# Second-pass w2 parts written one by one into w1's places of the first pass, block 0's last tiles spread over the first slot, w1 stores and weight sums at other times

## The chip, the cores and the metric

One Trainium2 chip; the kernel runs on one of its cores. The metric is the device time of one execution in microseconds (us), the median of several runs.

## The reference, cut to what matters

```python
# attention: 4 batches x 8 heads, 576 positions, head size 64
scores = where(mask, q @ k.T / 8, -1e9)   # heads 0-3: last 32 positions; heads 4-7: every 4th of the last 128
x = (softmax(scores) @ v)                 # gathered to [2304, 512]
# mixture of 4 experts, all used, weighted by p
p = domain_probs / (domain_probs.sum(-1, keepdims=True) + 1e-9)
for e in range(4):
    h = maximum(x @ w1[e], 0)             # [2304, 512] @ [512, 1024]
    out += p[:, e:e+1] * (h @ w2[e])      # [2304, 1024] @ [1024, 512]
```

## The kernel before, in words

The tokens lie in three blocks of 768 (`TB`), the 4 x 1024 hidden columns in 16 units `u` of 256. Every product is done in split precision: an operand is a high part in fp32r and a low part (the rest), and three matmuls (high by high, low by high, high by low) stand for one. The first layer uses a Strassen-like scheme with seven products per unit: w1 of a unit is turned into seven 256 x 128 pieces (A11, A12, A22 and the sums S1 to S4), x into seven pieces (B11 to T4).

**First pass.** While attention is still computing blocks 1 and 2, `experts` takes block 0 through all 16 units. For a unit, `w1_split` makes the high and low parts of A11, A12, A22 (tiles `g1h`, `g1l`, two buffers each; ScalarE makes the high part, GpSimd the low part), `w1_sums` makes the sums in place on GpSimd, `w1_late` splits the sums (`g2h`, `g2l`, one buffer each) and fetches the raw w1 of unit u+2 (tag `r1`, two buffers). `w2_late` splits the unit's w2 (raw tile `r2`, parts `w2h`, `w2l`) and fetches the next raw w2. `mm1_a` and `mm1_b` do the seven products, `mm2` the second layer: six output tiles of 128 tokens by 512, six matmuls each, in four PSUM banks, added up with the weight p by `weigh_out` (VectorE, L593). `keep_w1` (L218) stores the seven split pieces of a unit to DRAM in four DMAs, for the second pass. All these loads and stores are issued by SyncE's one queue, in program order, and an issue whose source or place isn't ready holds all behind it. ScalarE, VectorE, GpSimd and TensorE also take their instructions in program order.

**Second pass.** `second_pass` takes blocks 1 and 2 through the units in pairs: 16 groups of (pair, block), and a loop of 17 *slots*. A slot has seven steps b = 0 to 6. In it stand the first layer of group n (14 products `m1`, L501, six matmuls each, from pieces loaded back by `load_w1`, L709) and, between them, the second layer of group n-1 (seven products P1 to P7 by `m2`, L825). The seven w2 parts of a pair are made by the generator `w2_parts`: it fetches two raw w2 tiles (L847), and at each step makes a sum on GpSimd (L861 to L874), a high part on ScalarE (L855) and a low part on GpSimd (L856). `background(b)` takes one such step in most steps b, and one step of `w1_again`, which does for units 0 and 1 what `keep_w1` did for the others (sum L895, high part L897, low part L898, store L900).

In slot 0 there is no group before, so in its steps 0, 1 and 2 the last six tiles of block 0's second layer are done, two each. After step 2 `first_over` closes the pools of the first pass, and opens in their space the pool `late`, with the seven w2 parts, the raw w2 tiles, the places of the h pieces and the accumulators of blocks 1 and 2; the steps of the first `w2_parts` stand in b = 3 to 6, two in each.

Of the kernel before, what the change touches and what calls it, by code (L numbers as in the profile page):

```python
# [48 lines left out]
def kernel(  # L49
# [119 lines left out]
    def w1_sums(u):  # L169

        r = raw1[u]
        a11, a12 = r[:, 0:2, 0:128], r[:, 2:4, 0:128]
        a21, a22 = r[:, 0:2, 128:256], r[:, 2:4, 128:256]
        flush()
        tt = nc.gpsimd.tensor_tensor
        tt(out=a22, in0=a21, in1=a22, op=ALU.add)
        yield
        tt(out=a21, in0=a11, in1=a21, op=ALU.subtract)
        yield
        tt(out=a11, in0=a22, in1=a11, op=ALU.subtract)  # L180
        yield
        tt(out=a12, in0=a12, in1=a11, op=ALU.subtract)
        yield

    def w1_late(u):
        r = raw1.pop(u)
        gh = wp.tile([128, 4, 2, 128], F32R, tag="g2h", name="g2h")
        gl = wp.tile([128, 4, 2, 128], F32R, tag="g2l", name="g2l")
        ready1[u] += (gh, gl)
        for i, (n, c, f) in enumerate(  # L190
            (("S2", 0, 0), ("S1", 2, 128), ("S3", 0, 128), ("S4", 2, 0))
        ):
            v = (slice(None), slice(c, c + 2), slice(f, f + 128))
            split(gh[:, i], gl[:, i], r[v], nc.gpsimd if u > 2 else nc.vector)
            a_op[u, n] = (gh[:, i], gl[:, i])
            yield
        if u + 2 <= LAST:
            fetch_w1(u + 2)

    def w2_late(u):  # L200
        r = raw2.pop(u)
# [7 lines left out]
            fetch_w2(u + 1)  # L209


    def keep_w1(u):

        kept[u] = dram.tile([NO, 128, 2, FU], F32, name=f"w1_{u}")
        g1h, g1l, g2h, g2l = ready1.pop(u)
        for side, tiles in enumerate(((g1h, g2h), (g1l, g2l))):
            for at, t in zip((slice(0, 3), slice(3, NO)), tiles):
                nc.sync.dma_start(  # L218
                    out=kept[u][at, :, side, :].rearrange("n p f -> p n f"),
                    in_=t.bitcast(F32).rearrange("p n c f -> p n (c f)"),  # L220
                )

    b_op = {}

# [396 lines left out]
    def experts(begin):  # L621
# [35 lines left out]
        for i, (u, _) in enumerate(visits):  # L657
            end = u == LAST
            need(w1_late, u)
            keep_w1(u)  # L660
            yield from mm1_b((u, 0))
            if end:
                for n in ("T3", "T4"):
                    for j in (4, 5):
                        prepare(x_part, j, n)
                break
            prepare(w1_late, u + 1)
            if u + 2 <= LAST:
                prepare(w1_split, u + 2)
                prepare(w1_sums, u + 2)  # L670
            need(w1_split, u + 1)
            opening = mm1_a((u + 1, 0))
            yield next(opening)
            need(w2_late, u)
            yield from mm2((u, 0), False, False, 1)
            begin()
            yield from opening
            if u + 1 == LAST:

                assert "m1" in gate  # L680
                need(x_sums, 5)
                for n in ("T2", "T1"):
                    for j in (4, 5):
                        prepare(x_part, j, n)
            yield from mm2((u, 0), False, False, 0)
            if u + 2 <= LAST:
                prepare(w2_late, u + 2)
# [151 lines left out]
                    out=out[tt * 128:(tt + 1) * 128, d], in_=acc_t[g.m][:, at, d]  # L839
                )  # L840

    def w2_parts(pair):

        raw = []
        for u in pair:
            r = pools["late"].tile([128, 2, DM], F32, tag="r", name="r", bufs=2)
            nc.sync.dma_start(out=r, in_=w2_rows(u))  # L847
            raw.append(r)
        yield
        one, two = slice(0, DM // 2), slice(DM // 2, DM)  # L850
        b11, b12, b21, b22 = (r[:, :, d] for r in raw for d in (one, two))

        def split2(n, src):
            h, l = w2s[n][:, 0], w2s[n][:, 1]
# [12 lines left out]
        split2("P3", b22)  # L867
        yield
        tt(out=b12, in0=b22, in1=b12, op=ALU.subtract)
        split2("P7", b12)  # L870
        yield
        split2("P2", b21)
        yield
        tt(out=b21, in0=b21, in1=b11, op=ALU.add)  # L874
        split2("P4", b21)
        yield

    def w1_again(u):
# [9 lines left out]
        for n, src, one, two, op in (  # L888
# [17 lines left out]
    def second_pass(tiles):  # L906
# [11 lines left out]
        def first_over():  # L918
# [7 lines left out]
            for n in ORDER:  # L926
                w2s[n] = late.tile([128, 2, 2, DM // 2], F32R, name=f"w2_{n}")
            for at, names in enumerate((("S1", "S4"), ("S2", "A12"))):
                place = tuple(
                    late.tile([128, 2, TH], F32R, name=f"h{at}{i}") for i in ("h", "l")  # L930
                )
                for n in names:
                    h_places[n] = place

        g = h = w2_steps = None
        for n in range(len(groups) + 1):
            h, g = g, Group(n) if n < len(groups) else None

# [9 lines left out]
            def mm2_(b):  # L948
                if h:
                    m2(h, ORDER[b])  # L950
                elif b < 3:
                    for _ in range(2):
                        next(tiles)
                if n == 0 and b == 2:
                    assert next(tiles, 0) == 0
                    first_over()

            def background(b):
                nonlocal w2_steps
# [462 lines left out]
```

## Time and profile before

| what | us |
|---|---|
| median of 3 runs | 828.93 (828.52 to 831.21) |
| the profiled execution | 833.97 |
| its span, first to last instruction | 832.2 |
| TensorE busy | 800.9 (96%) |
| VectorE busy | 600.9 (72%) |
| GpSimd busy | 368.0 (44%) |
| ScalarE busy | 347.3 (42%) |
| mean granted TensorE clock | 0.984 |

Times in the profile count from the first instruction of the profiled execution. An idle time in square brackets stands before the instruction of its row, with what ended it. TensorE is the engine that is nearly always busy, so its idle time and the stretches in which its granted clock is under 1.00 are what to look for.

### The profile page before, as it was taken

To read this page: it belongs to the slowest core of one execution; us is meant where nothing else is said; L and a number is where in the kernel's file an instruction comes from. 1 tells how busy PE (TensorE), PEld (TensorE's weight loads), DVE (VectorE), ACT (ScalarE), POOL (GpSimd) and SP (SyncE) were. 2 spreads that over 40 slices of the span, in tenths; PEclk is the share of its full clock that TensorE was granted. 3 is DMA by queue.
4 is the path that set the end of the run, shared out by engine and by line. 5 is a ranking of instruction groups with operands and counts; after the bars stand their busy time and mean duration, and the time that the engine had idled before them with its cause. 6 is when DMAs were issued, how large, how long until landed. Compare 5 with 4: busy or idle time off the path is not lost.

```text
span 832.2 us, 17899 instructions
## 1 busy us (share of the span) xinstructions
PE 800.9 (96%) x7020; PEld 752.2 (90%) x7020; DVE 600.9 (72%) x1249; ACT 347.3 (42%) x707; POOL 368.0 (44%) x367
## 2 busy tenths in 40 slices
PE   8999799999999999599999999999999999999997
PEld 5878688888888889499999999999999999999997
DVE  4787456666665786367887777777886887877977
ACT  2555255454445534233443443442443432433432
POOL 4446578887776883330431631640520511502500
PEclk9999899999999999879999999999999999999999
DMA  7755675877555845535456456455454454454432
GB/s 221 233 154 136 221 249 174 261 218 218 174 172 171 278 153 179 179 94 176 127 171 197 145 156 206 139 158 173 125 171 124 125 172 124 125 178 127 128 108 95
DMA packets 101230, 140.08 MB, mean 168 GB/s; under 512 B 7561, under 2 KB 61705, under 8 KB 101147
## 3 DMA queue, kind: packets, MB, share of 16 engines
q1 hardware_dynamic: 100731, 138.51, 53.8%
q8 instruction: 56, 0.92, 0.4%
q10 hardware_dynamic: 416, 0.43, 0.1%
q14 instruction: 27, 0.22, 0.1%
HBM read 104.83 MB, written 34.08 MB: 167 GB/s over the span
## 4 chain that ended last, share of the span: by engine, by line
PE 84%; POOL 5%; DVE 5%; issue 3%; ACT 2%; DMA 1%; DVEq 0%; POOLq 0%; SPq 0%; ACTq 0%
PE m1x L501 24%; PE m L612 15%; PE m1y L501 15%; PE x L825 14%; PE y L825 11%; PE po L415 2%; POOL w_P L856 2%; PE sc L326 2%; DMA r<-w 1%; DVE acc L593 1%; PE wt L1177 1%; PE pt L395 1%; DVE xr L253 1%; DVE g L807 1%; POOL r L895 1%
## 5 line engine op out<-in xcount | busy, mean ns | idle before, releaser
L856 POOL TENSOR_TENSOR w_P<-r,w_P 128x512 fp32r<-128x512 f32 x56 | 75.9, 1357 | 259.8 <-PE m1y L501 164.0
L593 DVE SCALAR_TENSOR_TENSOR acc<-m,pn,acc 128x512 f32<-128x512 f32 x90 | 67.1, 748 | 39.2 <-PE m L612 39.1
L612 PE MATMUL m<-w2h,hh 128*128 128x512 f32 x192 | 77.9, 406 | 5.5 <-DVE acc L593 5.5
L807 DVE SCALAR_TENSOR_TENSOR g<-g 128x768 f32<-128x768 f32 x64 | 78.1, 1220 | 0.5
L612 PE MATMUL m<-w2l,hh 128*128 128x512 f32 x192 | 75.7, 394 | 0.0
L593 DVE SCALAR_TENSOR_TENSOR acc<-x,pn,acc 128x256 f32<-128x256 f32 x174 | 73.0, 473 | 0.9 <-PE x L825 0.9
L791 DVE TENSOR_TENSOR h0l<-g,h0h 128x768 fp32r<-128x768 f32 x32 | 36.7, 1146 | 45.2 <-ACT h0h L779 45.2
L593 DVE SCALAR_TENSOR_TENSOR acc<-y,pn,acc 128x256 f32<-128x256 f32 x138 | 58.0, 474 | 13.7 <-PE y L825 13.1
L501 PE MATMUL m1x<-xh_B,s_A 128*128 128x384 f32 x256 | 66.2, 340 | 0.0
L825 PE MATMUL x<-w_P,xh_T 128*128 128x256 f32 x384 | 61.5, 282 | 0.0
L825 PE MATMUL y<-w_P,h0h 128*128 128x256 f32 x384 | 61.3, 282 | 0.0
L612 PE MATMUL m<-w2h,hl 128*128 128x512 f32 x192 | 60.3, 395 | 0.4 <-DVE hl L525 0.4
L501 PE MATMUL m1y<-xh_B,s_S 128*128 128x384 f32 x192 | 49.9, 341 | 8.8 <-ACT g L763 8.8
L855 ACT ACTIVATE w_P<-r 128x512 fp32r<-128x512 f32 x56 | 34.9, 627 | 53.4 <-POOL r L861 21.1
L825 PEld LDWEIGHTS y<-w_P,h0h 128*128 128x128 f32 x384 | 54.2, 189 | 0.1
L825 PEld LDWEIGHTS x<-w_P,xh_T 128*128 128x128 f32 x384 | 54.3, 189 | 0.0
L501 PE MATMUL m1x<-xh_T,s_S 128*128 128x384 f32 x192 | 50.2, 342 | 3.5 <-DVE g L761 2.1
L612 PEld LDWEIGHTS m<-w2h,hh 128*128 128x128 f32 x192 | 36.3, 189 | 14.9 <-DVE acc L593 7.6
L138 POOL TENSOR_TENSOR g2l<-r,g2h 128x256 fp32r<-128x256 f32 x52 | 39.4, 770 | 22.3 <-ACT g2h L141 22.0
L771 ACT ACTIVATE g<-m1x 128x384 f32<-128x384 f32 x32 | 15.7, 492 | 74.0 <-PE m1x L501 74.0
L501 PEld LDWEIGHTS m1x<-xh_B,s_A 128*128 128x128 f32 x256 | 46.2, 190 | 0.1
L138 POOL TENSOR_TENSOR g1l<-r,g1h 128x256 fp32r<-128x256 f32 x45 | 34.0, 762 | 23.7 <-ACT g1h L141 23.7
(203 smaller groups left out, 2263.6 us busy)
## 6 DMA issues: line engine op xcount, KB each, us to landing
s_S<-w SPq DMA_DIRECT2D x128, 256.0 KB, 2.9
r<-w SPq DMA_DIRECT2D x49, 512.0 KB, 4.3
s_A<-w SPq DMA_DIRECT2D x96, 256.0 KB, 3.0
v_s<-vw SPq DMA_DIRECT2D x48, 192.0 KB, 4.8
w<-g2h SPq DMA_DIRECT2D x14, 512.0 KB, 5.4
w<-g2l SPq DMA_DIRECT2D x14, 512.0 KB, 6.2
w<-g1h SPq DMA_DIRECT2D x14, 384.0 KB, 4.8
w<-g1l SPq DMA_DIRECT2D x14, 384.0 KB, 5.9
```

What stands on the lines that cost most here:

```text
L138: lo_eng.tensor_tensor(out=lo, in0=src, in1=hi.bitcast(F32), op=ALU.subtract)
L326: nc.tensor.matmul(banks[swap][o:o + QB, i * KB:(i + 1) * KB], q_s[h, c0:c0 + QB], k_s[h, c0:c0 + KB], start=True, stop=True, skip_group_c ...
L415: nc.tensor.matmul(po[k][64 * j:64 * j + 64, o:o + QB], v_s[rows, j, 2 * i + half, :], ts_[rows, c:c + QB], start=True, stop=True,)
L501: nc.tensor.matmul(bank, w[:, k], x[:, k], start=(first and k == 0 and i == 0), stop=(last and k == 1 and i == 2), skip_group_check=True,)
L593: nc.vector.scalar_tensor_tensor(out=acc, in0=po, scalar=pn[:, tt, e:e + 1], in1=acc, op0=ALU.mult, op1=ALU.add,)
L612: nc.tensor.matmul(po, h, w, start=(n == 0 and x == 0), stop=(n == 3))
L771: copy(out=g.h[v, 0][:, 1], in_=to, func=AF.Copy)
L791: nc.vector.tensor_tensor(out=l, in0=source(g, n), in1=h.bitcast(F32), op=ALU.subtract)
L807: nc.vector.scalar_tensor_tensor(out=g.h[n], in0=g.h[one], scalar=0.0, in1=g.h[two], op0=ALU.max, op1=op)
L825: nc.tensor.matmul(to, h_places[factor][low][:, c, t * 128:(t + 1) * 128], w[:, x, c], start=begins and k == 0 and t != 1, stop=k == len(o ...
L855: nc.scalar.activation(out=h, in_=src, func=AF.Copy)
L856: nc.gpsimd.tensor_tensor(out=l, in0=src, in1=h.bitcast(F32), op=ALU.subtract)
```

## The change

- **Places.** The pool `wp` (raw and split weights of the first pass) stays open to the end, and only `fp` is closed. The two raw w2 tiles of a pair take the two `r1` buffers of raw w1; the parts are written one by one to `r2` (P1), `g2h` (P5), `g2l` (P6), the `w2h` and `w2l` of the unit before the last (P3, P7) and of the last (P2, P4). The places of the h pieces become `g1h` and `g1l`.
- **Fetch.** The raw w2 of the first pair is fetched by `w1_late` of units 14 and 15, where no w1 is left to fetch; later pairs in steps 2 and 3 of an odd slot.
- **First slot.** One tile of block 0 at each of b = 1 to 6, `first_over` after b = 6; w2 parts at b = 0 to 4, the last two in steps 0 and 1 of slot 1.
- **Stores.** A unit's `g1h` and `g1l` are stored when `w1_sums` begins, its `g2h` and `g2l` before `mm1_b` (for unit 2 after it).
- **Sums.** In `w2_parts` a sum is made at the end of the step before the one that splits it; in `w1_again` a step of its own lies between sum and split.

```diff
+    wp = ctx.enter_context(tc.tile_pool(name="wp", bufs=1))
     first_pass = ExitStack()
     fp = first_pass.enter_context(tc.tile_pool(name="fp", bufs=1))
-    pools = {}
-    wp = first_pass.enter_context(tc.tile_pool(name="wp", bufs=1))
...
     def w1_sums(u):
         flush()
+        keep_w1(u, False)
...
     def w1_late(u):
         if u + 2 <= LAST:
             fetch_w1(u + 2)
+        else:
+            fetch_w2_half(pairs2[0][u + 2 - NU])
...
-            keep_w1(u)
+            if u > 2:
+                keep_w1(u, True)
             yield from mm1_b((u, 0))
+            if u == 2:
+                keep_w1(u, True)
...
+    W2_PLACES = {
+        "P1": "r2", "P5": "g2h", "P6": "g2l", "P3": "w2h", "P7": "w2l", "P2": "w2h", "P4": "w2l",
+    }
...
+    def fetch_w2_half(u):
+        r = wp.tile([128, 2, DM], F32, tag="r1", name="r", bufs=2)
+        nc.sync.dma_start(out=r, in_=w2_rows(u))
+        raw_pair.append(r)
...
         split2("P1", b11)
+        tt(out=b11, in0=b12, in1=b11, op=ALU.subtract)
         yield
-        tt(out=b11, in0=b12, in1=b11, op=ALU.subtract)
         split2("P5", b11)
+        tt(out=b11, in0=b11, in1=b22, op=ALU.subtract)
         yield
-        tt(out=b11, in0=b11, in1=b22, op=ALU.subtract)
         split2("P6", b11)
...
     def w1_again(u):
             if op is not None:
                 tt(out=src, in0=one, in1=two, op=op)
+                yield
...
             def mm2_(b):
                 if h:
                     m2(h, ORDER[b])
-                elif b < 3:
-                    for _ in range(2):
-                        next(tiles)
-                if n == 0 and b == 2:
+                elif b:
+                    next(tiles)
+                if n == 0 and b == 6:
                     assert next(tiles, 0) == 0
                     first_over()
...
             def background(b):
-                if n == 0:
-                    if b == 3:
-                        w2_steps = w2_parts(pairs2[0])
-                        next(w2_steps)
-                    for _ in range(2 if b > 2 else 0):
-                        next(w2_steps, 0)
-                elif odd and b == 2 and q + 1 < len(pairs2):
-                    w2_steps = w2_parts(pairs2[q + 1])
-                    next(w2_steps)
-                elif not odd and b > 0 or odd and b < 2:
+                if n == 0 and b < 5 or n and not odd and b > 0 or odd and b < 2:
                     next(w2_steps, 0)
+                elif odd and q + 1 < len(pairs2):
+                    if b in (2, 3):
+                        fetch_w2_half(pairs2[q + 1][b - 2])
+                    elif b == 6:
+                        w2_steps = w2_parts()
```

**ScalarE in slot 0**, from the copy of the first product on (g and m1x, m1y are first-layer results and their banks, w2_P1 a w2 part, r its raw tile, xh_B22 the place of an h piece). Before:

```order
L759 ACTIVATE g_4715<-m1x_4714 128x384
L763 ACTIVATE g_4752<-m1y_4751 128x384
L765 ACTIVATE g_4752<-m1x_4742 128x384
L759 ACTIVATE g_4842<-m1x_4841 128x384
L1002 ACTIVATE g_4752<-g_4752 128x768
L771 ACTIVATE g_4715<-m1x_4742 128x384
L855 ACTIVATE w2_P1_4822<-r_4860 128x512
L855 ACTIVATE w2_P5_4823<-r_4860 128x512
L779 ACTIVATE xh_B22_0_934<-g_4715 128x768
L763 ACTIVATE g_4881<-m1y_4880 128x384
L855 ACTIVATE w2_P6_4824<-r_4860 128x512
```

And now:

```order
L765 ACTIVATE g_4719<-m1x_4718 128x384
L872 ACTIVATE w2_P1_4737<-r_4490 128x512
L769 ACTIVATE g_4742<-m1y_4741 128x384
L771 ACTIVATE g_4742<-m1x_4728 128x384
L872 ACTIVATE w2_P5_4768<-r_4490 128x512
L872 ACTIVATE w2_P6_4797<-r_4490 128x512
L765 ACTIVATE g_4801<-m1x_4800 128x384
L1015 ACTIVATE g_4742<-g_4742 128x768
L777 ACTIVATE g_4719<-m1x_4728 128x384
L872 ACTIVATE w2_P3_4828<-r_4643 128x512
L785 ACTIVATE xh_B22_0_934<-g_4719 128x768
L769 ACTIVATE g_4853<-m1y_4852 128x384
```

P1 stood behind six other instructions and now stands behind one; P5 and P6 now stand ahead of the copy of the eighth product (g_4801).

**SyncE's queue about units 2 and 3** (w1_2 is unit 2's store in DRAM, r1 and r2 raw w1 and w2). Before:

```order
L125 DMA r1_1500<-w1 128x4x256
L218 DMA w1_2_1504<-g1h_1306 128x3x256
L218 DMA w1_2_1504<-g2h_1450 128x4x256
L218 DMA w1_2_1504<-g1l_1307 128x3x256
L218 DMA w1_2_1504<-g2l_1451 128x4x256
L311 DMA v_s_1518<-vw 64x2x384 x2
L311 DMA v_s_1521<-vw 64x2x384 x2
L301 DMA q_s_1524<-qT 128x384
L302 DMA k_s_1525<-kT 128x2x224
L301 DMA q_s_1528<-qT 128x384
L302 DMA k_s_1529<-kT 128x2x224
L129 DMA r2_1532<-w2 128x2x512
```

And now:

```order
L125 DMA r1_1503<-w1 128x4x256
L314 DMA v_s_1516<-vw 64x2x384 x2
L314 DMA v_s_1519<-vw 64x2x384 x2
L304 DMA q_s_1522<-qT 128x384
L305 DMA k_s_1523<-kT 128x2x224
L304 DMA q_s_1526<-qT 128x384
L305 DMA k_s_1527<-kT 128x2x224
L129 DMA r2_1530<-w2 128x2x512
L221 DMA w1_3_1608<-g1h_1532 128x3x256
L221 DMA w1_3_1608<-g1l_1533 128x3x256
L221 DMA w1_2_1328<-g2h_1453 128x4x256
L221 DMA w1_2_1328<-g2l_1454 128x4x256
```

Unit 2's four stores stood ahead of unit 3's raw w2; two of them now stand a few issues before these rows (ahead of one v, q and k), two behind the raw w2, after unit 3's first two.

**GpSimd in slot 4** (r is raw w2, r1 the raw w1 of `w1_again`, again its split piece). Before:

```order
L856 TENSOR_TENSOR w2_P1_4822<-r_5688,w2_P1_4822 128x512
L861 TENSOR_TENSOR r_5688<-r_5688 128x2x256
L856 TENSOR_TENSOR w2_P5_4823<-r_5688,w2_P5_4823 128x512
L895 TENSOR_TENSOR r1_5599<-r1_5599 128x2x128
L898 TENSOR_TENSOR again_6007<-r1_5599,again_6007 128x256
L864 TENSOR_TENSOR r_5688<-r_5688,r_5690 128x2x256
L856 TENSOR_TENSOR w2_P6_4824<-r_5688,w2_P6_4824 128x512
```

And now:

```order
L912 TENSOR_TENSOR r1_5598<-r1_5598 128x2x128
L873 TENSOR_TENSOR w2_P1_4737<-r_5687,w2_P1_4737 128x512
L877 TENSOR_TENSOR r_5687<-r_5687 128x2x256
L916 TENSOR_TENSOR again_5960<-r1_5598,again_5960 128x256
L873 TENSOR_TENSOR w2_P5_4768<-r_5687,w2_P5_4768 128x512
L880 TENSOR_TENSOR r_5687<-r_5687,r_5734 128x2x256
L873 TENSOR_TENSOR w2_P6_4797<-r_5687,w2_P6_4797 128x512
```

A sum stood at the head of a step, right before the high part on ScalarE and the low part on GpSimd that are made from it; now it stands at the end of the step before, and the low part of `again` comes a step after its sum.

## Rows read from the trace of the kernel before

**Rows 1.** The page: busy time by engine, and TensorE in 40 slices.

```profile
PE 800.9 (96%) x7020; PEld 752.2 (90%) x7020; DVE 600.9 (72%) x1249; ACT 347.3 (42%) x707; POOL 368.0 (44%) x367
...
PE   8999799999999999599999999999999999999997
```

**Rows 2.** Windows in slot 0: length, busy PE, PEld, DVE, ACT, POOL, clock, DMA.

```profile
340.50:349.50 9.00, 0.20 (x2) 0.00 (x0) 0.39 (x1) 2.37 (x4) 3.60 (x3) 0.77 0.55 194
349.50:363.40 13.90, 11.76 (x43) 10.74 (x44) 7.69 (x7) 5.65 (x10) 11.52 (x9) 0.53 0.23 77
```

**Rows 3.** Timeline of TensorE in slot 0: start, duration, instruction, [idle before <-releaser].

```profile
349.51 1.01 PE L501 MATMUL m1y<-xh_B,s_S 128*128 128x384 f32 x2 [8.81 <-ACT g L763]
```

**Rows 4.** Timelines of SyncE's queue and of ScalarE in slot 0.

```profile
337.96 0.94 SPq L847 DMA_DIRECT2D r<-w  x2
...
344.38 0.63 ACT L855 ACTIVATE w_P<-r 128x512 fp32r<-128x512 f32 x1 [6.23 <-DMA r<-w]
```

**Rows 5.** Chain of waits in slots 0 and 1: start, duration, what ran.

```profile
320.87 1.06 PE m1x L501 x6
321.93 2.76 PE m L612 x12
...
365.60 2.14 PE y L825 x18
```

**Rows 6.** Timelines of ScalarE and VectorE at slot 0's first products.

```profile
324.94 0.49 ACT L759 ACTIVATE g<-m1x 128x384 f32<-128x384 f32 x1 [1.68 <-DVE xl_T L138]
...
326.07 0.54 DVE L761 TENSOR_TENSOR g<-m1x,g 128x384 f32<-128x384 f32 x1
```

**Rows 7.** GpSimd's L861 (ns min/median/max); GpSimd's and VectorE's timelines in slot 5.

```profile
L861 POOL TENSOR_TENSOR r<-r x8: 1262/1885/1886, 346.4 to 763.8; 128x512 f32<-128x512 f32 x8
...
484.12 0.75 POOL L898 TENSOR_TENSOR again<-r,again 128x256 fp32r<-128x256 f32 x1 [0.53 <-ACT again L897]
...
485.69 2.05 DVE L807 SCALAR_TENSOR_TENSOR g<-g 128x768 f32<-128x768 f32 x1
```

**Rows 8.** Windows in the first pass, unit 2 to 3, columns as in Rows 2.

```profile
93.40:98.70 5.30, 0.01 (x1) 0.00 (x0) 1.51 (x3) 3.09 (x8) 2.39 (x2) 0.77 0.21 81
98.70:103.20 4.50, 4.49 (x12) 3.90 (x13) 1.36 (x2) 0.00 (x0) 3.88 (x6) 0.52 0.41 129
```

**Rows 9.** Timeline of SyncE's queue ahead of unit 3's raw w2.

```profile
80.14 0.51 SPq L218 DMA_DIRECT2D w<-g1h  x1
...
83.79 4.02 SPq L311 DMA_DIRECT2D v_s<-vw  x4
...
90.01 9.51 SPq L129 DMA_DIRECT2D r<-w  x2
```

**Rows 10.** Timelines of VectorE, ScalarE and TensorE about that stall.

```profile
90.76 0.56 DVE L542 TENSOR_TENSOR s<-m1y,s 128x384 f32<-128x384 f32 x1 [0.38 <-PE m1y L501]
...
95.60 1.15 ACT L141 ACTIVATE w2h<-r 128x512 fp32r<-128x512 f32 x2 [9.55 <-DMA r<-w]
...
98.71 0.80 PE L612 MATMUL m<-w2h,hh 128*128 128x512 f32 x1 [5.30 <-DVE acc L593]
```

**Rows 11.** The page, DMA issues: count, KB each, median us to landing.

```profile
r<-w SPq DMA_DIRECT2D x49, 512.0 KB, 4.3
...
w<-g2l SPq DMA_DIRECT2D x14, 512.0 KB, 6.2
```

**Rows 12.** Waits from 400 us on: total us, times, longest.

```profile
ACT w_P L855 <- POOL r L861: 18.4, 7, 2.6
...
ACT again L897 <- POOL r L895: 15.3, 6, 3.5
...
PE m1x L501 <- DVE g L761: 5.0, 4, 1.5
```

**Rows 13.** Window over slots 4 to 7, columns as in Rows 2.

```profile
450.00:571.00 121.00, 116.01 (x812) 114.45 (x811) 90.71 (x147) 50.05 (x88) 46.78 (x40) 1.00 0.54 166
```

**Rows 14.** Waits over the whole span: total us, times, longest.

```profile
ACT w2h L141 <- DMA r<-w: 10.5, 2, 9.5
```

More of the change, by code (lines that the diff above doesn't have):

```diff
@@ L83 @@
     )
+    pools = {}
+    wp = ctx.enter_context(tc.tile_pool(name="wp", bufs=1))
     first_pass = ExitStack()
     fp = first_pass.enter_context(tc.tile_pool(name="fp", bufs=1))
-    pools = {}
-    wp = first_pass.enter_context(tc.tile_pool(name="wp", bufs=1))
     ident = const.tile([128, 128], F32, name="ident")
@@ L209, in w2_late, with keep_w1 @@
             fetch_w2(u + 1)
[L212 to L221, printed above, removed]
+    def keep_w1(u, late):
+        if not late:
+            kept[u] = dram.tile([NO, 128, 2, FU], F32, name=f"w1_{u}")
+        at = slice(3, NO) if late else slice(0, 3)
+        for side, t in enumerate(ready1[u][2:] if late else ready1[u][:2]):
+            nc.sync.dma_start(
+                out=kept[u][at, :, side, :].rearrange("n p f -> p n f"),
+                in_=t.bitcast(F32).rearrange("p n c f -> p n (c f)"),
+            )
     b_op = {}
@@ L840, in m2, with w2_parts @@
                 )
[L842 to L849, printed above, removed]
+    W2_PLACES = {
+        "P1": "r2", "P5": "g2h", "P6": "g2l", "P3": "w2h", "P7": "w2l", "P2": "w2h", "P4": "w2l",
+    }
+    raw_pair = []
+    def fetch_w2_half(u):
+        r = wp.tile([128, 2, DM], F32, tag="r1", name="r", bufs=2)
+        nc.sync.dma_start(out=r, in_=w2_rows(u))
+        raw_pair.append(r)
+    def w2_parts():
         one, two = slice(0, DM // 2), slice(DM // 2, DM)
-        b11, b12, b21, b22 = (r[:, :, d] for r in raw for d in (one, two))
+        b11, b12, b21, b22 = (r[:, :, d] for r in raw_pair for d in (one, two))
+        raw_pair.clear()
         def split2(n, src):
+            if n not in w2s:
+                tag = W2_PLACES[n]
+                w2s[n] = wp.tile(
+                    [128, 2, 2, DM // 2], F32R, tag=tag, name=f"w2_{n}",
+                    bufs=2 if tag[0] == "w" else 1,
+                )
             h, l = w2s[n][:, 0], w2s[n][:, 1]
@@ L867, in w2_parts @@
         split2("P3", b22)
+        tt(out=b12, in0=b22, in1=b12, op=ALU.subtract)
         yield
-        tt(out=b12, in0=b22, in1=b12, op=ALU.subtract)
         split2("P7", b12)
@@ L872, in w2_parts @@
         split2("P2", b21)
+        tt(out=b21, in0=b21, in1=b11, op=ALU.add)
         yield
-        tt(out=b21, in0=b21, in1=b11, op=ALU.add)
         split2("P4", b21)
@@ L925, in first_over @@
             pools["late"] = pools["acc"] = late
-            for n in ORDER:
-                w2s[n] = late.tile([128, 2, 2, DM // 2], F32R, name=f"w2_{n}")
             for at, names in enumerate((("S1", "S4"), ("S2", "A12"))):
                 place = tuple(
-                    late.tile([128, 2, TH], F32R, name=f"h{at}{i}") for i in ("h", "l")
+                    wp.tile([128, 2, TH], F32R, tag=f"g1{i}", name=f"h{at}{i}", bufs=2)
+                    for i in ("h", "l")
                 )
@@ L933, in first_over @@
                     h_places[n] = place
-        g = h = w2_steps = None
+        g = h = None
+        w2_steps = w2_parts()
         for n in range(len(groups) + 1):
@@ L960, in background @@
                 q, odd = divmod(n, 2)
-                if n == 0:
-                    if b == 3:
-                        w2_steps = w2_parts(pairs2[0])
-                        next(w2_steps)
-                    for _ in range(2 if b > 2 else 0):
-                        next(w2_steps, 0)
-                elif odd and b == 2 and q + 1 < len(pairs2):
-                    w2_steps = w2_parts(pairs2[q + 1])
-                    next(w2_steps)
-                elif not odd and b > 0 or odd and b < 2:
-                    next(w2_steps, 0)
+                if n == 0 and b < 5 or n and not odd and b > 0 or odd and b < 2:
+                    next(w2_steps, 0)
+                elif odd and q + 1 < len(pairs2):
+                    if b in (2, 3):
+                        fetch_w2_half(pairs2[q + 1][b - 2])
+                    elif b == 6:
+                        w2_steps = w2_parts()
                 if n > 2 and again and next(again[0], 0) == 0:
```

## The prediction

> **What bounds the kernel now.** I read the busy times first, then the windows, then the timelines of the places where TensorE idles. TensorE is busy 800.9 us of 832.2 and no other engine over 72% (PEld is its own weight load), so the work of TensorE is the floor; the 31 us in which it idles, and the time that it runs at half clock, are all that a change of order can win [rows 1]. In the slices the reader is to see a 7 in the fifth (83 to 104 us) and a 5 in the seventeenth (333 to 354 us) among nines. Both lie where the diff works, and the waits show a third place there that is too short for a slice.
>
> *Slot 0, the hand-over between the passes.* From 340.5 us on TensorE works 0.2 us in 9.0, and for the 13.9 us behind that its granted clock is 0.53, about 1.2 GHz in place of 2.4 [rows 2]. It waits for ScalarE's copy L763 [rows 3]. ScalarE was free, but ahead of that copy in its queue stands the high part of P1, and this waits for raw w2, which SyncE issues only at 337.96, when the first pass's space is given up; it is there at 344.4 [rows 4]. The parts behind it wait for GpSimd's sums in turn, with the copies that TensorE needs in between.
>
> *Unit 2 to 3 of the first pass.* TensorE idles 5.30 us from 93.4 and then runs 4.5 us at a clock of 0.52 [rows 8]. It waits for a PSUM bank, the bank for VectorE, VectorE for ScalarE's `hh`, and ScalarE for unit 3's raw w2: the copy L141 idled 9.55 us, to 95.60, because of that load [rows 10]. The load was issued at 90.01, behind the four stores of unit 2 (80.14 to 83.79), four issues of v (4.02 us) and two each of q and k [rows 9].
>
> *Slots 4 to 7.* TensorE idles 5.0 us in four stalls, all before a product that waits for VectorE's L761 [rows 12], at clock 1.00 throughout [rows 13]. VectorE is late there because ScalarE had waited for GpSimd sums: 18.4 us in all for L861, 15.3 us for L895 [rows 12].
>
> **The change part by part.** The sum is made against the profiled execution, 833.97 us; its median runs are 5.0 us shorter, and I take the saving off the median as it is.
>
> *A. Slot 0.* From the end of the product at 340.5 to where the clock is full again, at 363.4, 22.9 us pass. In them lie four products and P1: 4 x 1.06 + 2.14 = 6.4 us at full clock [rows 2, 3, 5]. So 16.5 us are to be won at most. What must be there instead: raw w2 is fetched by `w1_late` of units 14 and 15, and the later of these stands ahead of unit 15's `mm1_b`, five products or 5.3 us before slot 0 [rows 5]; at 4.3 us a load [rows 11] both halves are in before slot 0's first copy at 324.94 [rows 6]. No place of P1 to P7 is late either: the last one to be stored, `g2l` of unit 15, lands 6.2 us after its issue [rows 11], about 1 us into slot 0, and P6 is due some 10 us later. P2 and P4 wait for the last tile, but stand in slot 1, and are read only in its steps 5 and 6.
>
> Two new waits I see. First, four tiles (4 x 1.38, from 2.76 for two) stood between the second product and the fourth; now one does [rows 5]. The fourth adds into a bank that VectorE's L761 must have read, and L761 needs ScalarE's first copy, which ran only at 324.94 since it waited for x parts whose space it takes [rows 6]. So L761 ends at 324.94 + 0.49 + 0.54 = 326.0 or a little later, and TensorE is there at 320.87 + 3 x 1.06 + 1.38 = 325.4: a new stall of 0.7 us. Second, P5 and P6 stand on ScalarE ahead of the copy that frees the bank of the ninth product. Their chain starts when P1's high part ends, 0.63 us behind the first copy, at 326.1: low part, sum, P5's high part, low part, sum, P6's high part, copy. With the four GpSimd operations at 1.26 us, two high parts (0.63), the copy (0.49) and some 0.1 us for each hand-over it ends at 333.4; with 1.88 us each [rows 7] at 335.9. TensorE wants the bank at 326.1 + 5 x 1.06 + 2 x 1.38 = 334.2. I take 0.3 us, nearer to the short end, since slot 0 has no second layer of a group before, whose VectorE work surrounds the long ones. So A is 16.5 - 0.7 - 0.3 = 15.5 us. Ends: 16.5, and 12.1 with 3.7 for the second wait: 1.7 for the bank, and 1 us each at two products behind a VectorE add that is late as L807 was [rows 7].
>
> Why some are 1.26 and some 1.88: the sum L861 has both in this trace, and VectorE's L807 took 2.05 us beside such a sum [rows 7]. The Trainium skill, SBUF — State Buffer, section "SBUF: two separate sides", says that GpSimd and a VectorE instruction with two SBUF inputs take a shared port pair as an exclusive lock, so that the later one blocks fully. That speaks against putting w2's parts beside a slot that VectorE fills; followed to its end it is the third rival below.
>
> The tiles themselves cost the same wherever they stand. The six output stores that now stand apart in SyncE's queue each wait for their eviction, which comes before the next product ends: nothing.
>
> *B. Unit 2 to 3.* Two of the four stores now go out earlier, when the queue is empty, and two behind the raw w2. The load moves up by what the four cost the queue, 83.79 - 80.14 = 3.65 us, to 86.4 [rows 9]; the four v issues may shrink too, as less traffic is under way. At 4.3 us [rows 11] it is there at 90.7, while ScalarE's next instruction needs VectorE's L542 at 90.76 + 0.56 anyway [rows 10]. So the stall of 5.30 goes but for 0.5 us, and with it the half clock: six matmuls of a tile and six of a product took 4.5 us and take 1.38 + 1.06 = 2.44 at full clock [rows 5, 8], 2.06 us. What is late next: the two late stores of unit 2 must land before unit 3's `g2h` and `g2l` are written. Behind the raw w2 and unit 3's first two stores, at some 0.5 us an issue [rows 9], they go out at about 87.8 and 88.3, and with 6.2 us on the way the second lands at 94.5, as TensorE ends the third tile (93.4 + 0.5 + 1.38) and asks for the first of these parts at 95.3. I take B as 5.3 + 2.06 - 0.5 = 6.9 us; ends 7.4 and 0.
>
> *C. Sums one step ahead.* A step is some 4.2 us long (two products and one w2 product, 2 x 1.06 + 2.14); GpSimd's three operations in it are mostly no more than 1.88 + 1.88 + 0.75 [rows 7], with 1.26 in place of 1.88 where VectorE isn't in the way. So a sum that ends its step is nearly always done when the next begins, ScalarE's two waits go, and the four stalls with them: 5.0 us at most, 0 at least. I take 4.5. The extra steps end in slot 8, long before units 0 and 1 are read back.
>
> *D. The other visits of the first pass.* The same stores in another order, beside TensorE's work, which waits for none of them before; 0, with the rivals as bounds.
>
> Sum: 15.5 + 6.9 + 4.5 = 26.9 us. 833.97 - 26.9 = 807.1 for a profiled execution, and **828.93 - 26.9 = 802.0** for the median.
>
> **The rivals.**
>
> 1. *The late stores take the place of the load.* `g2h` and `g2l` of unit 2 have one buffer, and their stores now share the DMA engines with the raw w2 and unit 3's first stores. If they land 4 us later than I reckon, TensorE stalls 4 us before unit 3's S2 product and pays 2 us of half clock as it did at 98.7 [rows 8]: B falls to 0.9, the time to 808.0. For it: the same traffic in the same 10 us. Against: 0.8 us are in hand even so, and more if SyncE's issues of v take less time.
>
> 2. *The hole stays in slot 0.* If one place isn't free when its part is due (a store or a raw half over 10 us late), P5 or P6 blocks the copies as P1 did at 344. Then A is lost but for some 3 us: 828.93 - 3 - 11.4 = 814.5. Against it: stores and halves have several us in hand (A), and no such load took over 6.4 us in this stretch [rows 4].
>
> 3. *GpSimd and VectorE block each other in slot 0.* The second wait of A is then at its long end, 3.7 us in three pieces in place of 0.3. Stalls of 1.5 us left the clock at 1.00 [rows 12, 13], so nothing is added: 802.0 + 3.4 = 805.4. This is what the rule of the skill's page gives if every meeting is a full block; the trace agrees with it in the two durations of L861, and shows that not each operation meets one.
>
> 4. *Slower: the early stores hold up the queue in each visit.* The stores of `g1h` and `g1l` now stand in SyncE's queue ahead of q, k, v and of raw weights, and wait for GpSimd's splits. If in a visit a raw w2 comes as late as in unit 3, that visit costs 7.4 us (B's whole). There are thirteen such visits; from four on (29.6 us) the gain of 26.9 is gone: 828.93 + 2.7 = 831.6. Against it: ScalarE's waits for a raw load are 10.5 us in the whole span, 9.5 of them the one stall [rows 14]; in all other visits the load has time in hand, and it already waited for the later of GpSimd's splits, so that a store that waits for an earlier one adds little.
>
> **How the numbers follow.** My forecast (A, B, C within a few tenths to 2 us) gets 0.64: 802.0, by itself 799 (all three at their upper ends, 16.5 + 7.4 + 5.0 = 28.9, and 1 us more) to 805. Rival 1 has 0.15, rival 3 0.12, rival 2 0.05, rival 4 0.04. The range takes in rivals 1 and 3, and both together (802.0 + 6.0 + 3.4 = 811.4): 799 to 812. Rival 2 and the slower one are left outside, and some of the odd mixtures. A measurement of this kernel can tell about 0.3% from no change, 2.5 us (the three runs lie that far apart). Rivals 1 to 3 are all faster by more: faster 0.95. Rival 4 gives slower 0.03, and 0.02 for no change, when it takes about as much as the rest gives.
>
> **What would show it.** Right: TensorE's slices are at 9 from 333 to 374 us; no wait for L763 in slot 0; P1's high part runs right after the first copy; the stall before unit 2's third tile is under 1 us and the clock there 1.00; in slots 4 to 7 ScalarE waits no more for L861's and L895's successors and the four stalls before L761's product are gone. A new stall of about 1 us stands before slot 0's fourth product. Wrong: a wait of ScalarE or GpSimd for a store of `g2h` or `g2l`, in slot 0 or at unit 3; a stretch at half clock near 325 to 345 us; waits for raw w1 or w2 that recur from visit to visit.

## The result, and the profile after

The change is faster: **804.95 us** (804.73 to 806.31, 4 runs) beside 830.07 us (828.52 to 831.49, 4 runs) of the kernel before; ratio 0.9701, 95% interval 0.9677 to 0.9726. Forecast were 802.0, range 799 to 812. The profiled execution took 804.96 us, span 803.2.

The page of the changed kernel, busy times and TensorE's slices, to be read against [rows 1]: TensorE is busy 9 us less, though the matmuls are the same 7020, and the 7 and the 5 among the nines are gone.

```profile
PE 791.8 (99%) x7020; PEld 746.2 (93%) x7020; DVE 601.7 (75%) x1249; ACT 347.4 (43%) x707; POOL 375.7 (47%) x367
...
PE   8999999999999999999999999999999999999997
```

Its windows (length, busy PE, PEld, DVE, ACT, POOL, clock, DMA): the stretch of unit 2 to 3, slot 0 with the product before it and the start of slot 1, and slots 4 to 7; below them slots 4 to 7 of the kernel before, cut at the same instructions.

```profile
92.00:98.00 6.00, 5.06 (x36) 3.82 (x42) 1.91 (x3) 3.20 (x9) 4.64 (x7) 1.00 0.48 165
...
314.00:326.00 12.00, 11.32 (x59) 10.18 (x58) 6.40 (x10) 5.60 (x12) 8.38 (x7) 1.00 0.62 207
326.00:345.00 19.00, 19.00 (x117) 18.20 (x116) 15.20 (x22) 7.58 (x14) 8.29 (x6) 1.00 0.62 202
...
426.90:545.80 118.90, 118.90 (x843) 118.90 (x842) 98.23 (x152) 49.96 (x89) 49.29 (x38) 1.00 0.54 169
...
450.30:575.50 125.20, 120.21 (x843) 118.66 (x842) 94.21 (x152) 50.62 (x90) 46.78 (x40) 1.00 0.54 164
```

The clock column says 1.00 in all of them; [rows 2, 8] had 0.53 and 0.52 in the first two places. In slots 4 to 7, whose clock was at 1.00 before too [rows 13], the same 843 matmuls took 125.2 us before and take 118.9 now.

TensorE's waits over the whole span of the changed kernel (us in total, times, longest). Of the three places that [rows 3, 10, 12] showed, these are left:

```profile
PE m1y L504 <- POOL g2l L138: 0.7, 1, 0.7
PE m1x L504 <- DVE g L767: 0.7, 1, 0.7
...
PE m L615 <- DVE acc L596: 0.2, 1, 0.2
```

To see where the time came from I cut the span at instructions that every version has: the scores (L329, 96 matmuls) ahead of unit 2's stall and the next ones ("unit 2 to 3"), the first product of slot 0, and the first matmul of P1 in each slot. Lengths are differences of their starts in the traces, in us:

| kernel | unit 2 to 3 | slot 0 to P1 of slot 1 | slots 4 to 7 | span |
|---|---|---|---|---|
| before | 33.9 | 39.5 | 125.2 | 832.2 |
| after | 27.8 | 24.9 | 118.8 | 803.2 |
| e1 slot 0 only | 33.4 | 24.9 | 125.1 | 817.0 |
| e2 old stores | 33.4 | 25.0 | 118.8 | 808.5 |
| e3 no step in `w1_again` | 28.2 | 24.9 | 129.2 | 814.4 |
| e4 old sums in `w2_parts` | 27.8 | 24.9 | 118.8 | 804.3 |
| e5 two tiles a step | 27.7 | 28.4 | 118.8 | 805.1 |
| e6 raw pair late | 28.6 | 32.4 | 118.8 | 810.7 |
| e7 all of unit 2's stores early | 32.7 | 24.9 | 118.8 | 806.7 |
| e8 earlier load, tiles 0 to 5 | 31.3 | 25.3 | 118.8 | 807.6 |
| e9 swap | 26.5 | 25.1 | 118.8 | 800.0 |
| e9 no tile in step 3 | 28.0 | 24.1 | 118.8 | 801.9 |
| e9 both | 27.0 | 24.3 | 118.8 | 804.1 |

The change saves 6.1, 14.6 and 6.4 us in the three, and 1.0 us in slot 1 (30.7 to 29.7), whose first 2.2 us had run at half clock too (0.50 from 360.2 to 362.4 us of the kernel before, in the second window of [rows 2]): with their rounding 28.0 of the 29.0 us between the spans. Slots 1 to 14 now take 29.7 us each.

**Unit 2 to 3.** Timelines of the changed kernel: SyncE's queue, ScalarE, GpSimd, TensorE.

```profile
79.10 2.48 SPq L314 DMA_DIRECT2D v_s<-vw  x4
...
83.78 0.41 SPq L129 DMA_DIRECT2D r<-w  x1
84.29 0.41 SPq L221 DMA_DIRECT2D w<-g1h  x1
85.05 0.38 SPq L221 DMA_DIRECT2D w<-g1l  x1
85.79 0.36 SPq L221 DMA_DIRECT2D w<-g2h  x1
86.20 0.92 SPq L221 DMA_DIRECT2D w<-g2l  x1
...
89.42 1.16 ACT L141 ACTIVATE w2h<-r 128x512 fp32r<-128x512 f32 x2 [4.43 <-DMA r<-w]
...
92.94 1.34 ACT L141 ACTIVATE g2h<-r 128x256 fp32r<-128x256 f32 x4 [1.95 <-DMA w<-g2h]
...
94.34 2.80 POOL L138 TENSOR_TENSOR g2l<-r,g2h 128x256 fp32r<-128x256 f32 x4 [1.36 <-ACT g2h L141]
...
92.55 0.50 PE L615 MATMUL m<-w2h,hh 128*128 128x512 f32 x1 [0.20 <-DVE acc L596]
...
95.12 0.44 PE L504 MATMUL m1y<-xh_T,g2l 128*128 128x384 f32 x1 [0.74 <-POOL g2l L138]
```

The raw w2 is issued at 83.78 instead of 90.01 [rows 9], and ScalarE's copy runs at 89.42 instead of 95.60 [rows 10]; 1.0 us of each difference is that this execution reached the stretch sooner. The late stores now hold `g2h`'s place: ScalarE waits 1.95 us for one, and TensorE 0.74 behind it.

**Slot 0.** Timelines of ScalarE, VectorE, GpSimd and TensorE of the changed kernel.

```profile
317.14 0.49 ACT L765 ACTIVATE g<-m1x 128x384 f32<-128x384 f32 x1 [1.67 <-PE m L615]
317.52 0.62 ACT L872 ACTIVATE w_P<-r 128x512 fp32r<-128x512 f32 x1
...
324.38 0.63 ACT L872 ACTIVATE w_P<-r 128x512 fp32r<-128x512 f32 x1 [2.78 <-POOL r L880]
324.92 0.47 ACT L765 ACTIVATE g<-m1x 128x384 f32<-128x384 f32 x1
...
317.66 0.56 DVE L767 TENSOR_TENSOR g<-m1x,g 128x384 f32<-128x384 f32 x1 [0.64 <-ACT g L765]
...
319.64 1.29 POOL L877 TENSOR_TENSOR r<-r 128x512 f32<-128x512 f32 x1
...
328.90 2.02 POOL L885 TENSOR_TENSOR r<-r 128x512 f32<-128x512 f32 x1
...
318.27 0.61 PE L504 MATMUL m1x<-xh_T,s_S 128*128 128x384 f32 x2 [0.68 <-DVE g L767]
```

P1's high part follows the first copy without a wait for its raw tile. The copy behind P5 and P6 runs at 324.92, with no stall of TensorE behind it.

**Slots 4 to 7.** ScalarE's waits of the changed kernel from 400 to 560 us:

```profile
ACT w_P L872 <- POOL r L877: 7.6, 3, 2.6
...
ACT again L915 <- POOL r L912: 1.6, 2, 0.8
```

From 400 us to the end the first is 15.5 us in 6 waits, beside 18.4 in 7 [rows 12], so a single wait is no shorter; over the whole span it is 19.0 us in 8, and was 21.1 in 8 (the expectation of e3 sets 19.0 against 18.4, which do not cover the same stretch). Only the second, 15.3 us there, is nearly gone. So which edit removed TensorE's four stalls was open.

### The profile page after: what moved, and what is told of

It reads as the page before. It is cut to its first block, busy times and chain, and to the rows that moved or that the text cites. A ratio compares the mean times of both kernels' runs of the same rounds, so it can differ in the third digit from the quotient of the medians.

```text
span 803.2 us, 17909 instructions
## 1 busy us (share of the span) xinstructions
PE 791.8 (99%) x7020; PEld 746.2 (93%) x7020; DVE 601.7 (75%) x1249; ACT 347.4 (43%) x707; POOL 375.7 (47%) x367
## 4 chain that ended last, share of the span: by engine, by line
PE 92%; DVE 3%; DMA 1%; ACT 1%; issue 1%; POOL 0%; SPq 0%; DVEq 0%; POOLq 0%; ACTq 0%
PE m1x L504 27%; PE x L831 17%; PE m1y L504 16%; PE m L615 15%; PE y L831 13%; PE po L418 2%; PE sc L329 1%; PE wt L1190 1%; PE pt L398 1%; DMA w<-g2h 1%; DVE acc L596 1%; DMA v_s<-vw 1%; DVE sm L343 1%; DVE hl L528 0%; ACT hh L522 0%
## 5 line engine op out<-in xcount | busy, mean ns | idle before, releaser
L797 DVE TENSOR_TENSOR h0l<-g,h0h 128x768 fp32r<-128x768 f32 x32 | 37.3, 1166 | 39.4 <-ACT h0h L785 39.4
L138 POOL TENSOR_TENSOR g2l<-r,g2h 128x256 fp32r<-128x256 f32 x52 | 39.8, 778 | 23.4 <-ACT g2h L141 21.1
L138 POOL TENSOR_TENSOR g1l<-r,g1h 128x256 fp32r<-128x256 f32 x45 | 34.9, 785 | 21.1 <-ACT g1h L141 21.1
```

What stands on the lines that cost most here:

```text
L138: lo_eng.tensor_tensor(out=lo, in0=src, in1=hi.bitcast(F32), op=ALU.subtract)
L797: nc.vector.tensor_tensor(out=l, in0=source(g, n), in1=h.bitcast(F32), op=ALU.subtract)
```

## The experiments

My theory: three parts that add up, each a wait of ScalarE ahead of a copy that TensorE needs. The rivals are with each run. None leaves out a part of the computation. Line numbers in the experiments differ from those of the changed kernel by a few.

**The parts.** e2 puts the stores back, e3 takes the step out of `w1_again`, e4 puts the sums of `w2_parts` back, and e1 does all three, which leaves places, fetch and tiles of slot 0.

```diff
e2
     def w1_sums(u):
         flush()
-        keep_w1(u, False)
...
-            if u > 2:
-                keep_w1(u, True)
+            keep_w1(u)
             yield from mm1_b((u, 0))
-            if u == 2:
-                keep_w1(u, True)
e3
                 tt(out=src, in0=one, in1=two, op=op)
-                yield
e4 (and so at each sum)
         split2("P1", b11)
-        tt(out=b11, in0=b12, in1=b11, op=ALU.subtract)
         yield
+        tt(out=b11, in0=b12, in1=b11, op=ALU.subtract)
         split2("P5", b11)
```

> The changed kernel with the stores of w1 and all sums as they were before: only the new places, the early fetch and the spread tiles are left. My theory, that the three parts add up (15.8 us slot 0, 6.1 the stall between units 2 and 3, 5.6 the sums, read from the two traces): 804.95 + 11.7, some 815 to 818 us, with the 5.3 us stall before unit 2's third tile and the four stalls in slots 4 to 7 back. Rival, that the other two stalls were chance of one execution or hang on the places: 804 to 808 us.

Measured: 818.19 us (816.02 to 819.94), ratio 0.9832 (0.9799 to 0.9865), just above the range. Slot 0 has its whole gain, and the four stalls of slots 4 to 7 (1.03, 1.45, 1.03, 1.51 us) and the one of unit 2 (4.8) are back: the parts are separate.

> The changed kernel with the stores of w1 in their old place in SyncE's queue. My theory: unit 3's raw w2 is late again, TensorE idles about 5 us before unit 2's third tile and runs some 4 us at half clock: 804.95 + 6, some 810 to 812 us. Rival, that the order of the stores is worth nothing and the load was late for another reason: 805 us, with no stall over 1 us there.

Measured: 810.38 us (808.80 to 810.49), ratio 0.9735 (0.9707 to 0.9763), as expected. Timeline of SyncE's queue in e2, and TensorE's wait:

```profile
81.40 1.42 SPq L220 DMA_DIRECT2D w<-g2l  x1
82.87 4.00 SPq L313 DMA_DIRECT2D v_s<-vw  x4
...
89.06 0.42 SPq L129 DMA_DIRECT2D r<-w  x1
...
PE m L614 <- DVE acc L595: 5.3, 1, 5.3
```

The stores cost the load 5.3 us: their own issues, and 1.5 us more for the four of v behind them, which took 2.48 us in the changed kernel.

> The changed kernel without the extra step in w1_again between a sum and its split (sums of w2_parts stay one step ahead). ScalarE's wait for the w2 sum L877 didn't shrink with the change (19.0 us after, 18.4 before), while its wait for w1_again's sum is gone. So my theory is that w1_again's step alone ended the four stalls of slots 4 to 7: 809 to 811 us here, with stalls of 1 to 1.5 us in these slots. Rival, that the sums of w2_parts did it: 805 us and no stalls.

Measured: 816.39 us (815.27 to 820.05), ratio 0.9822 (0.9780 to 0.9864): slower than the changed kernel as expected, but by 11 us where some 5 were. Slots 4 to 7 take 129.2 us, 4 more than in the kernel before. Timelines of GpSimd, ScalarE and TensorE in slot 4 of e3, and ScalarE's wait for this sum from 400 to 560 us:

```profile
442.19 1.29 POOL L880 TENSOR_TENSOR r<-r 128x512 f32<-128x512 f32 x1
443.44 0.74 POOL L912 TENSOR_TENSOR r<-r 128x256 f32<-128x256 f32 x1
...
444.21 0.42 ACT L914 ACTIVATE again<-r 128x256 fp32r<-128x256 f32 x1 [3.47 <-POOL r L912]
444.53 0.47 ACT L765 ACTIVATE g<-m1x 128x384 f32<-128x384 f32 x1
...
445.06 0.63 PE L504 MATMUL m1x<-xh_B,s_A 128*128 128x384 f32 x2 [0.89 <-ACT g L765]
...
ACT again L914 <- POOL r L912: 22.0, 6, 4.1
```

Put early, the sum L880 stands on GpSimd ahead of the sum L912, for which ScalarE waits in the same step. ScalarE's wait of 3.47 us ends with L912, the copy behind it comes late, and TensorE stalls. So the early sums of `w2_parts` alone do harm, and the step in `w1_again` undoes it.

> The changed kernel with the sums of w2_parts at the head of their step as before. My theory, as in the run without w1_again's step: this move is worth little in slots 4 to 7, 0 to 1 us there; in slot 0 P5's and P6's chain is no longer, since the sum only moves behind a step's end: 805 to 806.5 us. Rival, that the sums of w2_parts ended the four stalls: 809 to 811 us.

Measured: 804.89 us (803.33 to 807.05), ratio 0.9675 (0.9642 to 0.9708): no different from the changed kernel, and slots 4 to 7 all take 29.7 us. With the step in `w1_again`, where the sums of `w2_parts` stand makes no difference; ScalarE waits for them either way, with nothing urgent behind.

**Slot 0.** e5 keeps the tiles two in a step, as they were; e6 fetches the first raw pair at the head of slot 0, with the places of the changed kernel.

```diff
e5
-                elif b:
-                    next(tiles)
-                if n == 0 and b == 6:
+                elif b < 3:
+                    for _ in range(2):
+                        next(tiles)
+                if n == 0 and b == 2:
e6
-        else:
-            fetch_w2_half(pairs2[0][u + 2 - NU])
...
             def background(b):
                 q, odd = divmod(n, 2)
+                if n == 0 and b == 0:
+                    for u in pairs2[0]:
+                        fetch_w2_half(u)
```

> The changed kernel with block 0's last six tiles two each in slot 0's steps 0 to 2, as before; places, fetch and w2 parts as changed. My theory, that the early fetch and the separate places fill the hole and the spread is worth nothing by itself: from slot 0's first product to P1 24.9 us as in the changed kernel or 0.7 less (no stall before the fourth product, four tiles again in front of it); 804 to 805.5 us. Rival, that the tiles in the later steps are what covers GpSimd's chain of sums and parts: TensorE waits for ScalarE's copies behind P3 and P7, 3 to 5 us longer, 808 to 810 us.

Measured: 807.09 us (806.52 to 809.41), ratio 0.9724 (0.9697 to 0.9751). The theory, that the tiles' spread matters little, falls, and the rival was right, at a smaller price: slot 0 takes 3.4 us more. Timelines of ScalarE and TensorE in e5, and a window behind (columns as above):

```profile
333.40 0.63 ACT L872 ACTIVATE w_P<-r 128x512 fp32r<-128x512 f32 x1 [1.86 <-POOL r L885]
333.94 0.47 ACT L771 ACTIVATE g<-m1x 128x384 f32<-128x384 f32 x1
...
334.46 0.62 PE L504 MATMUL m1x<-xh_T,s_S 128*128 128x384 f32 x2 [1.36 <-ACT g L771]
336.73 1.01 PE L504 MATMUL m1x<-xh_T,s_A 128*128 128x384 f32 x2 [0.94 <-DVE g L775]
...
338.00:341.00 3.00, 3.00 (x15) 3.00 (x14) 0.69 (x1) 1.57 (x3) 0.00 (x0) 0.65 0.19 70
```

The stall before the fourth product is gone, with two tiles ahead of it. But from step 3 on there is nothing between the products; TensorE overtakes the chain of w2 parts, stalls twice, and its clock falls to about its half level behind.

> The changed kernel with both raw w2 tiles of the first pair fetched at the head of slot 0 in place of w1_late of units 14 and 15. My theory, that a raw tile that isn't there holds up the copies behind it on ScalarE: P1 runs some 3 to 5 us later, TensorE waits 2 to 4 us for the copy L769, 1 to 2 us of half clock may follow; 807 to 811 us. Rival, that the hole came from the space that was given up late and not from the load: the same 805 us.

Measured: 814.01 us (812.65 to 817.61), ratio 0.9809 (0.9776 to 0.9841): the mechanism as expected, the price larger. Timelines of ScalarE and TensorE in e6, and a window:

```profile
323.97 0.63 ACT L870 ACTIVATE w_P<-r 128x512 fp32r<-128x512 f32 x1 [5.62 <-DMA r<-w]
...
325.03 1.01 PE L502 MATMUL m1y<-xh_B,s_S 128*128 128x384 f32 x2 [4.71 <-ACT g L767]
...
325.00:332.00 7.00, 6.97 (x23) 6.39 (x24) 1.86 (x3) 1.62 (x3) 5.36 (x5) 0.60 0.49 170
```

This is the hole of [rows 3, 4] again, 4.71 us long instead of 8.81. At least half of slot 0's gain hangs on the early fetch: 7.5 of 14.6 us, with the load at the head of slot 0, where the kernel before had it only after step 2.

**The store order and what is left.** e7 issues unit 2's late stores ahead of `mm1_b`, like those of other units. e8 fetches unit u+1's raw w2 one step earlier in the queue and puts the tiles in steps 0 to 5.

```diff
e7
-            if u > 2:
-                keep_w1(u, True)
+            keep_w1(u, True)
             yield from mm1_b((u, 0))
-            if u == 2:
-                keep_w1(u, True)
e8
             w2_op[u, c] = (wh[:, c], wl[:, c])
+            if c and 1 < u < LAST:
+                fetch_w2(u + 1)
             yield
-        if 1 < u < LAST:
-            fetch_w2(u + 1)
...
-                elif b:
+                elif b < 6:
                     next(tiles)
-                if n == 0 and b == 6:
+                if n == 0 and b == 5:
```

> The changed kernel with the late stores of unit 2 in front of its mm1_b as for the other units, so ahead of q, k, v and of unit 3's raw w2. My theory, that the load is late by what stands ahead of it: half of the four stores, so that about half of the stall comes back, 2 to 3 us before unit 2's third tile with or without half clock: 807 to 809 us. Rival, that only the first two stores counted (the queue has room for the others), and the wait of 0.7 us for g2l before unit 3's S2 product goes: 804 us.

Measured: 807.55 us (805.73 to 810.90), ratio 0.9729 (0.9695 to 0.9763), as expected. The raw w2 goes out at 85.70, the third tile waits 3.2 us, and the clock is at about half behind (0.51 from 94 to 98 us). So the odd `if u == 2` carries most of this part's gain: 4.9 of 6.1 us.

> The changed kernel with the tiles in slot 0's steps 0 to 5 in place of 1 to 6 (two tiles ahead of the fourth product), and with unit u+1's raw w2 fetched one step of the queue earlier, so that unit 3's stands ahead of v, q, k. My theory: the stall of 0.68 us before the fourth product and that of 0.20 before unit 2's third tile go, about 1.3 us with what a restart costs: 803.5 to 804.2 us. Rival, that v, q, k, now behind the load, or the stores of g2h and g2l take the place: 805 us or more.

Measured: 807.32 us (803.99 to 809.33), ratio 0.9708 (0.9671 to 0.9745): a miss, and the rival was right. Timelines of ScalarE and TensorE in e8, and a window:

```profile
95.58 1.33 ACT L141 ACTIVATE g2h<-r 128x256 fp32r<-128x256 f32 x4 [4.06 <-DMA w<-g2h]
...
96.05 0.45 PE L504 MATMUL m1y<-xh_T,g2h 128*128 128x384 f32 x1 [1.56 <-ACT g2h L141]
97.75 0.44 PE L504 MATMUL m1y<-xh_T,g2l 128*128 128x384 f32 x1 [1.26 <-POOL g2l L138]
...
99.40:102.80 3.40, 3.40 (x76) 2.96 (x77) 0.00 (x0) 1.93 (x6) 1.74 (x3) 0.61 0.46 126
```

The load is early, at 80.63, and the late stores go out at 89.50 and 90.23; they become the bound. In slot 0 the step that now lacks a tile stalls 1.01 us before its product.

The last three take on the two stalls that are left: "swap" issues unit 2's late stores ahead of unit 3's early ones, still behind the load, "skip3" has its tiles in all steps but 3, and "both" has the two edits.

```diff
swap
     def w1_sums(u):
         flush()
+        if u == 3:
+            keep_w1(2, True)
         keep_w1(u, False)
...
-            if u == 2:
-                keep_w1(u, True)
skip3
-                elif b:
+                elif b != 3:
                     next(tiles)
```

> The change with unit 2's two late stores (g2h, g2l) issued ahead of unit 3's two early ones (g1h, g1l). In the changed kernel they went out at 85.79 and 86.20 us, behind g1h at 84.29 and g1l at 85.05, and TensorE stalled 0.20 us before unit 2's third tile and 0.74 us before unit 3's S2 product, which waited for GpSimd's g2l. Theory: the places of g2h and g2l come free about 1.5 us earlier, the 0.74 us go, with some 0.35 us for the restart; the stage from unit 2 to unit 3 falls from 27.8 to some 26.8, the time to about 803.9. Rival: the landing depends on the traffic of the raw load, not on the issue: the stall stays and the time is 804.9; or g1h and g1l, now later, hold the next writer of their places.

> The change with block 0's last six tiles in steps 0, 1, 2, 4, 5 and 6 of slot 0 in place of 1 to 6. Theory: two tiles (2.76 us) instead of one stand ahead of the fourth product, so its stall of 0.68 us goes with the 0.35 us of its restart, and a tile is left in step 6, whose lack cost a stall of 1.01 us in the version with tiles in 0 to 5; the bank of the ninth product keeps its margin, as five tiles still stand ahead of it or beside it. Slot 0 to P1 of slot 1 falls from 24.9 to 23.9 us, the time to about 803.9. Rival: without a tile in step 3 the product behind P6 comes 1.38 us earlier and waits for ScalarE's copy behind P6: a new stall of 0.5 to 1.4 us there, the time 804.9 or a little more.

> Both edits: theory 804.9 - 1.0 - 1.0 = 802.9 us; rival: whichever of the two stalls stays, 803.9 to 804.9.

Measured: 803.97 us (801.87 to 805.61), ratio 0.9653 (0.9626 to 0.9680); 804.73 us (801.92 to 807.11), ratio 0.9666 (0.9629 to 0.9704); and 804.04 us (802.58 to 805.86), ratio 0.9657 (0.9632 to 0.9681). TensorE's waits over the span of "both":

```profile
PE m L617 <- DVE acc L598: 0.3, 1, 0.3
```

Each edit removes its stall: unit 2 to 3 falls by 1.3 us with the swap, slot 0 by 0.8 with the other, and no new wait over 0.4 us appears. The medians moved by up to 1 us, less than the 3 to 5 us by which runs of one version differ here, and "both" is no faster than "swap" where 802.9 us were expected; that these versions beat the changed kernel is seen in the traces and not shown by the times.

The traces show where part of that spread lies. Up to the scores ahead of unit 2's stall these three versions do not differ from the changed kernel, yet this opening took 68.4 us in "swap", 69.7 in "skip3", 70.1 in the changed kernel and 72.4 in "both". From there to the end they took 731.6, 732.3, 733.1 and 731.7 us. Timeline of TensorE and a window, in "both":

```profile
23.73 1.62 PE L420 MATMUL po<-pts,v_s 64*64 64x32 f32 x46 [1.53 <-issue]
...
24.00:30.00 6.00, 6.00 (x100) 5.50 (x103) 2.42 (x4) 3.02 (x8) 1.01 (x1) 0.50 1.01 317
```

In "swap" TensorE stood 0.43 us before the same instruction, and the same window had the clock at 1.00. The profile doesn't show what TensorE waited for there.

## Why the prediction was right, and where it was off

**A, slot 0: right.** 15.5 us were forecast, 14.6 + 1.0 = 15.6 came. The raw halves and places were in time, the new stall before the fourth product was 0.68 us (0.7 forecast), and the bank of the ninth product cost nothing (0.3). That the sum came out to 0.1 us is in part luck: the 0.3 us too much stand against the restart behind the stall, which I had left out (see C). What I gave no price was the spread of the tiles ("cost the same wherever they stand"): true of their matmuls, but e5 shows that as cover for the chain of parts it is worth 3.4 us.

**B, unit 2 to 3: mechanism right, 0.8 us too much.** 6.9 forecast, 6.1 measured. The load went out 1.6 us before my 86.4, counted from the scores, since the issues of v shrank to 2.48 us; but it took 5.6 us (83.78 to 89.42) where I had 4.3, and so came hardly earlier than my 90.7. The rest of 0.5 us was mis-sized: it is 0.20 + 0.74 us of idle and the restarts behind them. I had asked only when the late stores land, and let the making of the parts behind them cost nothing: ScalarE's `g2h`, from 92.94, and GpSimd's `g2l`, from 94.34 and 0.7 us each, still stand ahead of the product. The second stall is rival 1 in small; in e8 it is larger, with half clock behind. My sign for "wrong", a wait for the store of `g2h` at unit 3, did appear, at 1.95 us.

**C, slots 4 to 7: the size and one reason were off.** 4.5 us forecast with an end at 5.0, 6.4 measured. The upper end was wrong because I read a stall's cost from its listed idle time: the four slots are 6.4 us shorter where 5.0 us were idle, so each stall cost (6.4 - 5.0) / 4 = 0.35 us more than its bracket. The windows of slots 4 to 7 say the same: for the same 843 matmuls TensorE was idle 5.0 us (125.20 - 120.21) and also busy 1.3 us longer (120.21 against 118.90). And "ScalarE's two waits go" was half wrong: the wait for the sums of `w2_parts` stayed, and e3 and e4 show that all came from the step in `w1_again`.

**D: no effect shown.** The stretch before the scores shrank by 1.0 us and that from unit 3 to slot 0 by 0.7, and the end, from P1 of slot 16 on, grew by 0.7. Versions that are the same there differ by as much: 68.4 to 72.4 us, 214.9 to 215.6, and 20.1 to 21.1. Rival 4 didn't come: ScalarE's waits for raw w2 in the first pass fell from 10.5 us [rows 14] to 4.4.

**Rivals 2 and 3.** The hole did not stay; e6 makes it come back. GpSimd and VectorE did not block each other where it counts: the operations up to P6 took 1.29 and 1.30 us. The Trainium skill, SBUF — State Buffer, section "SBUF: two separate sides", lets a meeting on the shared port pair block one side fully. The trace agrees for the 2.02 us of L885 above: it began 0.56 us into VectorE's L792, with two SBUF inputs (328.34 us, 1.43 us long), and 1.29 us counted from that one's end would end at 331.06, where it ended at 330.92. The sum L877 took 1.29 us in slot 0, beside no such operation, and 1.89 the other seven times, each begun beside a VectorE L797. No stall followed L885 in the changed kernel.

**From the sum to the median.** Against the profiled execution I forecast a saving of 26.9 us, and it was 29.0. The time is still 3 us above my 802.0, since I took the saving off the median "as it is". The profiled execution of the kernel before was 4 to 5 us over its median and that of the changed kernel is at its median, so between medians 25.1 us were saved. In 21 further executions of the kernel before, the mean granted clock lay between 0.979 and 0.989 and the time between 828.99 and 835.48 us, so the stalls or what follows them differ from run to run. Which of them did so in the kernel before is open, as only one of its executions was profiled; between profiled executions of the later versions the opening differs, as shown above.

## What to carry to other kernels

An in-order engine that is half idle can still set the time: look for what stands behind a wait in its queue, and judge the wait by that, not by its length. Two reorderings that meet in one queue have to be tried apart and together, as one may harm alone and be free beside the other. Where a load and a store compete for one queue, each early place is paid for by the other, and here the best order found lies between the extremes.

## What the runs showed of the hardware that I had not expected

- **A stall costs more than its idle time.** Some 0.35 us on top in slots 4 to 7, at a clock of 1.00. Part of it is seen in the rows: in an unbroken row of products a pair of matmuls takes 0.51 us, and the first pair behind a stall 0.61 to 0.63. The rest fits the last matmul before a stall, which is shown busy for its 0.34 us where the next would have started 0.17 us in.
- **Short stalls can be followed by half clock, and their length alone doesn't tell when.** Two close together, of 1.36 and 0.94 us (e5), ending 2.3 us apart, and of 1.56 and 1.26 (e8), ending 1.7 us apart, were followed by a granted clock of 0.65 and 0.61, near the 1.2 GHz level, in the windows shown. Single stalls of up to 1.51 us in slots 4 to 7 ([rows 12, 13] and e1) and the 0.20 and 0.74 us above left it at 1.00. But in the opening of the changed kernel a single stall of 1.22 us was followed by 3.4 us at 0.50, while 1.27 us before the same instruction in "swap" left the clock at 1.00. What tells these cases apart is not shown.

```profile
17.19 0.51 PE L418 MATMUL po<-pts,v_s 64*64 64x32 f32 x13 [1.22 <-issue]
...
17.40:20.80 3.40, 3.40 (x58) 2.26 (x54) 1.70 (x9) 1.01 (x2) 1.81 (x3) 0.50 0.85 248
```

- **An issue on SyncE's queue took longer right behind large stores.** Four issues of v took 2.48 us in the changed kernel, and 4.00 to 4.27 us right behind stores of `g2h` and `g2l` (before, e2, e7), the first two of them 1.3 to 1.6 us each. The cause is not shown.
